# Idle score strips take quarter-products of PV as 32x32 tiles, in a two-layer attention and MLP kernel

## The chip, the cores and the metric

The kernel runs on one core of one Trainium2 chip. The metric is the device time in microseconds (us), median over the runs. The core's engines have queues of their own: PE (matmuls, with PEld for the weight loads), ACT (activations), DVE and POOL (elementwise work), SP (DMA issue).

## What is computed

Two times the same pair of blocks over x of 2048 rows by 512, in bf16, with the same weights: attention with 32 heads of 16, then an MLP of width 1792.

```
x = x + A(layernorm(x));  x = x + B(layernorm(x))        # twice
A: q, k, v = split(x @ wqkv);  p = softmax(q k^T / 4);  (p @ v) @ wo
B: gelu(x @ w1 + b1) @ w2 + b2
```

A head has only 16 dimensions, so the matmuls of attention are small and the exponentials many: 2 x 32 x 2048 x 2048 of them.

## The kernel before

The kernel is a planner in Python: generators (`scores`, `exps`, `pvs`, `solo`, `hpair`, ...) yield operations with costs, `_Sched.run` picks at each step the operation that can start first on its engine by a clock of its own, and the result is one fixed order of instructions for each engine, with semaphore waits. A table of weights, `ROWS`, holds settings of the planner's rules, and `PIECES` says which row holds in each hundredth of the program.

Attention goes in passes. A pass is a layer, a block of 512 queries and four heads, one in each quarter of 128 channels (in the last blocks 256 queries and eight heads; `setup_attention`). Its unit of work is a cell `(pass, kt, a)`: 128 keys, the head in quarter `a`, 512 columns. In all there are 4096 cells. A cell's score (`score`, line 1598 of before) is a matmul with 32 rows of weights and 128 columns on row strip `a` of the array (tile position `(32a, 0)`). A **score phase** (mode "S") issues scores on two to four different strips; mostly it is three: two for ACT and one for DVE. Each goes to a bank of PSUM of its own.

A cell's exponentials come from one of two places. On ACT (`exps`, line 2234) one activation takes two or three cells, that is 1024 or 1536 columns, and writes `pt`. On DVE (`dfirst`, line 1867) one operation per cell makes integers whose bits read as bf16 approximate the exponential, and two shifted copies (POOL, line 2097) refine it, so that a cell on DVE gives three products to be added, where a cell on ACT gives one.

A **product** multiplies 128 keys of `p` with 17 columns of `v` (16 dimensions and a column of ones for the softmax's sum), at tile `(0, 32a)`: 128 rows by 32 columns. `pvs` (line 2301) issues rounds of four of them, one on each quarter of columns, into the one PV bank (`PVB`), which stays open over a pass (mode "P"). The projections and the MLP (line 715) have the same 128x32 shape. Where the plan has PE idle, `fill` puts in matmuls without use (line 1586).

`next_act` and `next_d` choose the cells of a phase; `op.late` is called when a phase's start is known and may add cells (`attach`, `more`); `op.apart` holds matmuls that go out in the same phase under a semaphore step of their own. The planner charges a phase or a round `MM`, and `SW` at each change between modes S and P.

Of the kernel before, what the change touches and what calls it, by code (L numbers as in the profile page):

```python
# [63 lines left out]
KWAIT = (140, 230, 320)  # L64
KSTEP = 10
# [30 lines left out]
         "CLOSE",)  # L96
ROWS = (
# [42 lines left out]
)  # L140
PIECES = (4, 23, 28, 27, 28, 25, 25, 25, 23, 25, 20, 25, 25, 25, 20, 20, 20, 24, 15, 36, 36, 30, 31, 24, 24, 24, 33, 33, 24, 24, 24, 0, 0,
          5, 5, 37, 25, 25, 6, 25, 14, 18, 30, 30, 3, 35, 37, 5, 19, 19, 5, 20, 38, 41, 38, 35, 35, 35, 35, 24, 17, 17, 17, 14, 19, 7, 7, 7,
          18, 18, 18, 39, 39, 22, 15, 1, 41, 41, 39, 41, 39, 25, 25, 2, 2, 14, 23, 25, 25, 35, 35, 32, 32, 34, 36, 32, 38, 41, 41, 32)
# [193 lines left out]
class _Sched:  # L337
# [169 lines left out]
    def run(self):  # L507
        while True:
# [62 lines left out]
            for f, r, w in op.apart:  # L571
                ev = self.P.group(e, [f], r, w)
                self.end[ev] = start + cost + op.tail + LATENCY[e]
# [131 lines left out]
class _Plan:  # L705
# [746 lines left out]
    def setup_attention(self):  # L1452
# [40 lines left out]
        self.slots = [list(x) for x in SLOTS]  # L1493
        self.held, self.users = [len(x) for x in SLOTS], [0] * len(SLOTS)
        self.dmine = {c for q in self.dlist for c in q}
        self.ended, self.pvopen, self.pvwas, self.hold = False, False, False, set()
        self.rush = self.base[(NL - 1, self.segs[-1][-3])]
        self.duleft, self.open, self.starved, self.lend = {}, None, 0, 2
        self.tbusy, self.s.tbusy = set(), None
# [101 lines left out]
    def next_act(self, used=()):  # L1601
        while self.pa < len(self.pas):
            for q in (self.alist[self.pa], self.dlist[self.pa]):
                if q:
                    return q.pop(next((k for k, c in enumerate(q) if c[2] not in used), 0))
# [816 lines left out]
```

## Time and profile before

| | |
|---|---|
| median of three runs | 1375.13 us (1374.58 to 1377.1) |
| the profiled execution | 1374.89 us, span 1373.1 us |
| busy in the span | PE 1338.8, ACT 1349.0, DVE 1261.8, POOL 802.8 us |
| matmuls | 18168, and as many weight loads |
| ACT's exponentials | start 12.2 us to 1343.8 us into the span |

A run's time is a little over its span. Busy times of an engine join instructions that overlap: an activation's recorded length contains the end of the one before, and a matmul's end is modelled. So distances from start to start tell more than lengths.

### The profile page before, as it was taken

The numbers are of one execution on the slowest core, as the hardware profiler recorded it, in microseconds if no ns is written. First come the engines' busy times: TensorE is split into PE (matmuls) and PEld (weight loads), VectorE is DVE, ScalarE is ACT, GpSimd is POOL, SyncE is SP. The second block draws the span as 40 slices with busy tenths as digits, with TensorE's granted clock in tenths as the row PEclk, the third lists the DMA queues.
The fourth block names the chain that finished last, engine by engine and source line by source line (L and its number), as shares of the span: only waits on it lengthen the run. The fifth ranks groups of instructions, "written<-read, shape, count | busy, mean of one in ns | idle before, by whom it ended". The sixth has DMA issues, their size and how long they took to land.

```text
span 1373.1 us, 42332 instructions
## 1 busy us (share of the span) xinstructions
PE 1338.8 (98%) x18168; PEld 390.1 (28%) x18168; DVE 1261.8 (92%) x2504; ACT 1349.0 (98%) x1385; POOL 802.8 (58%) x1352
## 2 busy tenths in 40 slices
PE   9999999999999999999999999999999999999999
PEld 3222222222222222222222222222222222333446
DVE  8999999989999899998979899999999898999894
ACT  7999999999999999999999999999999999999995
POOL 1367667657665567665626666546656665765461
DMA  5300000123221221112451141100104314201112
GB/s 149 72 2 1 2 2 23 49 75 97 71 43 45 89 83 55 44 51 65 114 109 40 49 128 57 48 17 12 37 24 117 93 40 143 83 14 44 29 34 83
DMA packets 122296, 80.20 MB, mean 58 GB/s; under 512 B 36732, under 2 KB 121084, under 8 KB 122108
## 3 DMA queue, kind: packets, MB, share of 16 engines
q1 hardware_dynamic: 122108, 77.49, 20.6%
q8 instruction: 143, 2.34, 0.7%
q14 instruction: 45, 0.37, 0.1%
HBM read 65.67 MB, written 4.19 MB: 51 GB/s over the span
## 4 chain that ended last, share of the span: by engine, by line
ACT 83%; PE 10%; DVE 6%; DMA 1%; issue 0%
ACT pt L2234 70%; PE ps L715 5%; ACT kt L2234 3%; ACT g L1276 3%; PE ps L1598 3%; ACT v L2234 2%; PE ps L2301 2%; DVE dp L1867 2%; ACT q L2234 2%; DVE kt L1867 1%; ACT L2234 1%; ACT L1276 1%; ACT g L2234 1%; DVE stats L848 0%; DMA wr<-in_B_w_dram 0%; DMA wr<-in_A_wqkv_dram 0%
## 5 line engine op out<-in xcount | busy, mean ns | idle before, releaser
L2234 ACT ACTIVATE pt<-ps 128x1024 bf16<-128x1024 f32 (+1 forms) x1183 | 1142.7, 1176 | 2.0 <-PE ps L1598 1.6
L1598 PE MATMUL ps<-qp,kt 32*128 32x512 bf16 x4096 | 551.5, 384 | 16.6 <-ACT pt L2234 12.2
L2097 POOL INT64_ADD dp<-dp x732 | 440.2, 613 | 204.8 <-DVE dp L1867 123.1
L1867 DVE TENSOR_SCALAR dp<-ps 128x512 uint16<-128x512 f32 x733 | 483.3, 679 | 26.3 <-PE ps L1598 23.4
L1598 PEld LDWEIGHTS ps<-qp,kt 32*128 32x128 bf16 x4096 | 138.4, 91 | 569.7 <-ACT pt L2234 466.7
L2097 POOL INT64_ADD kt<-kt x320 | 190.1, 599 | 174.1 <-DVE kt L1867 93.6
L2301 PE MATMUL ps<-pt,v 128*17 128x512 bf16 (+1 forms) x2758 | 273.9, 359 | 1.4 <-ACT pt L2234 0.7
L1867 DVE TENSOR_SCALAR kt<-ps 128x512 uint16<-128x512 f32 x309 | 207.4, 683 | 23.4 <-PE ps L1598 20.8
L2301 PE MATMUL ps<-dp,vc 128*17 128x512 bf16 (+1 forms) x1652 | 220.7, 357 | 0.6 <-POOL xf L2097 0.4
L2301 PE MATMUL ps<-dp,v 128*17 128x512 bf16 (+1 forms) x826 | 139.1, 357 | 3.4 <-DVE xt L1076 2.4
L2097 POOL INT64_ADD v<-v x155 | 94.1, 611 | 71.7 <-DVE v L1867 35.8
L715 PE MATMUL ps<-xf,wr 128*32 128x512 bf16 (+1 forms) x1888 | 134.6, 366 | 0.5 <-DVE g L1258 0.4
L2301 PE MATMUL ps<-kt,vc 128*17 128x512 bf16 (+1 forms) x766 | 117.6, 340 | 1.0 <-POOL xf L2097 0.3
L1867 DVE TENSOR_SCALAR v<-ps 128x512 uint16<-128x512 f32 x154 | 102.8, 682 | 13.2 <-PE ps L1598 12.8
L715 PE MATMUL ps<-wr,g 128*32 128x512 bf16 x1408 | 108.1, 384 | 0.5 <-DVE dp L1867 0.2
L2301 PEld LDWEIGHTS ps<-pt,v 128*17 128x17 bf16 x2758 | 69.8, 88 | 74.5 <-issue 51.8
L2301 PE MATMUL ps<-kt,v 128*17 128x512 bf16 (+1 forms) x507 | 85.8, 350 | 1.7 <-DVE xt L1076 1.0
L2097 POOL INT64_ADD xf<-xf x78 | 46.5, 596 | 65.5 <-DVE xf L1867 40.3
L1258 DVE TENSOR_SCALAR g<-ps,hb1t 128x512 bf16<-128x512 f32 (+1 forms) x112 | 78.9, 706 | 1.0 <-PE ps L715 1.0
L2301 PEld LDWEIGHTS ps<-dp,vc 128*17 128x17 bf16 x1652 | 56.7, 88 | 42.0 <-issue 24.4
L2234 ACT ACTIVATE kt<-ps 128x1024 bf16<-128x1024 f32 (+1 forms) x60 | 63.4, 1189 | 0.0
L2301 PE MATMUL ps<-v,vc 128*17 128x512 bf16 x308 | 60.8, 381 | 0.0
(124 smaller groups left out, 1425.5 us busy)
## 6 DMA issues: line engine op xcount, KB each, us to landing
wr<-in_B_w_dram SPq DMA_DIRECT2D x174, 256.0 KB, 2.9
wr<-in_A_wqkv_dram SPq DMA_DIRECT2D x24, 256.0 KB, 3.3
x<-in_A_x_dram SPq DMA_DIRECT2D x7, 512.0 KB, 4.3
wr<-in_A_wo_dram SPq DMA_DIRECT2D x10, 256.0 KB, 3.7
kept<-x SPq DMA_DIRECT2D x4, 512.0 KB, 3.1
x<-kept SPq DMA_DIRECT2D x4, 512.0 KB, 4.4
out_dram<-x SPq DMA_DIRECT2D x16, 128.0 KB, 2.5
q<-in_B_w_dram SPq DMA_DIRECT2D x3, 512.0 KB, 4.5
```

The lines of the kernel that those rows point to most:

```text
L715: return [lambda e, a=a: e.matmul(out[32 * a:32 * a + 32, :], lhsT=lhsT[:, 32 * a:32 * a + 32], rhs=rhs, start=start, stop=stop, tile_posi ...
L1258: yield _Op("dve", 0.21 + n / 966, lambda e, fc=fc, pb=pb: e.tensor_scalar(T["G"][:, fc, q], pb, T["HB1T"][:, fc:fc + 1], None, op0=ALU.ad ...
L1276: lambda e, g=g: e.activation(out=g, in_=g, func=ACT.Gelu_apprx_tanh), reads=gk, writes=gk, prio=2)
L1598: return (lambda e: e.matmul(o, lhsT=lhsT, rhs=rhs, start=True, stop=True, tile_position=(32 * a, 0)), ["K%d.%d.%d" % (l, gb, kt // 4), "Q ...
L1867: yield _Op("dve", 0.682, lambda e: e.tensor_scalar(u, self.bank(b), E_SCALE, E_BIAS, op0=ALU.mult, op1=ALU.add), reads=["B.%d" % b], writ ...
L2097: op = _Op("pool", PFIX + PWORD * 128 * (hi - lo), lambda e: e.int64_add(dst, src, by * PACKED), reads=reads, writes=writes)
L2234: yield _Op("act", EXPC + 0.4267 * n, lambda e, src=src, dst=dst: e.activation(out=dst, in_=src, func=ACT.Exp, scale=0.25), reads=["B.%d" ...
L2301: op.fns.append(lambda e, o=o, lhsT=q[0][0][m], rhs=q[0][1][:, n * m:n * m + n], a=a, st=st, sp=sp: e.matmul(o, lhsT=lhsT, rhs=rhs, start= ...
```

## The change

A score phase mostly leaves a row strip idle. The change lets that strip do a quarter of four products: 32 of the 128 keys of one product in each of the four column quarters, four matmuls on 32x32 tiles at `(32r, 32a)`, accumulated into the open PV bank. Such four matmuls are called a **unit** here. Four units, on four different strips in four different phases, finish four products, a round of `pvs` before. `beside` makes units: at most one between two phases of another mode, and each waits on PE's own semaphore for the unit before it. `avoid` steers the choice of cells so that the strip left idle is one that a begun set of four still lacks. `pvs` issues what is left at the end of a pass as units alone. The table of settings gets a new column and more rows, and `PIECES` is chosen anew.

```diff
+PARTS = 2
+PLEFT = 7
+STEER = 1
...
-    (0.5, 0.3, 0.7, 0.2, 10, 10, 2, 6, 1, 1, 2, 2, 5, 0.3, 0.4, 2, 3.5, 24, 3, 4, 0.4, 1.0, 0, 1, 2, 3, 1, 2, 0.3, 2, 0.15, 0.0, 0.35,),
+    (0.5, 0.3, 0.7, 0.2, 10, 10, 2, 6, 1, 1, 2, 2, 5, 0.3, 0.4, 2, 3.5, 24, 3, 4, 0.4, 1.0, 0, 1, 2, 3, 1, 2, 0.3, 2, 0.15, 0.0, 0.35, 7,),
...
-            for f, r, w in op.apart:
+            for f, r, w, *order in op.apart:
+                for x in order:
+                    for y in x:
+                        self.P.wait(e, *y)
                 ev = self.P.group(e, [f], r, w)
+                for x in order:
+                    x[:] = [ev]
...
+    def avoid(self):
+        parts = self.cur["parts"] if self.cur and STEER else []
+        left = set.union(*[x["left"] for x in parts]) if parts else set()
+        return left if parts and (len(parts) == PARTS or not self.cur["more"]) and len(left) < 3 else set()
...
+    def beside(self, op, start, cells):
+        if self.s.mode != "S":
+            self.laid = False
+        cur = self.cur
+        if cur is None or self.laid or not all(cur["begun"]):
+            return
+        idle = [r for r in range(4) if all(c[2] != r for c in cells)]
+        if not idle:
+            return
+        cur["more"] = min(self.pvleft[k] for k in cur["cols"]) >= PLEFT
+        part = next((x for x in cur["parts"] if x["left"] & set(idle)), None)
+        if part is None and cur["more"] and len(cur["parts"]) < PARTS:
...
+        r = next(r for r in idle if r in part["left"])
+        part["left"].discard(r)
+        op.apart.append((self.quarter(cur, part, r, len(cur["parts"]) == 1 and not part["left"] and not any(self.pvleft[k] for k in cur["cols"])),
+                         part["keys"], ["B.%d" % cur["b"]], self.order))
+        self.laid = True
...
+    def quarter(self, cur, part, r, end):
+        bank, n = self.bank(cur["b"]), cur["n"]
+        row = slice(32 * r, 32 * r + 32)
+
+        def f(e):
+            for m in range(512 // n):
+                for a, ws, p in part["work"]:
+                    x = e.matmul(bank[32 * a:32 * a + 17, n * m:n * m + n], lhsT=ws[m][row, :], rhs=p[row, n * m:n * m + n], start=False, stop=end and m == 512 // n - 1,
+                                 tile_position=(32 * r, 32 * a))
+            return x
+        return f
...
+                for r in sorted(x["left"]):
+                    op = _Op("pe", MM, [self.quarter(cur, x, r, i == len(cur["parts"]) - 1 and r == max(x["left"]))], reads=x["keys"], writes=["B.%d" % b], prio=0.5, mode="S")
+                    op.late = lambda op, start: self.P.wait("pe", "pe", self.P.cnt["pe"])
+                    yield op
+                    self.order[:] = [("pe", self.P.cnt["pe"])]
```

Lines move: the scores stand at 1647 in the changed kernel (1598 before), the rounds of PV at 2440 (2301), projections and MLP at 763 (715), the fillers at 1635 (1586), ACT's exponentials at 2372 (2234), DVE's at 2004 (1867). The units are line 1724.

What the built programs hold, counted in their order of instructions:

| | before | after |
|---|---|---|
| scores (line 1598, 1647) | 4096 | 4096 |
| cells on ACT, in activations of two cells and of three | 2769 in 1200 + 123 | 2756 in 1210 + 112 |
| cells on DVE | 1327 | 1340 |
| matmuls of fillers in the 128x32 and 128x17 shapes | 404 | 604 |
| matmuls of units, units | 0 | 3728 in 828 (104 of them in two halves of 256 columns) |
| places where 128-row and 32-row tiles follow each other | 2730 | 2682 |
| matmuls in all | 18168 | 21296 |

On PE of before, in the stretch where the hidden layer of an MLP block runs beside attention (`xf,wr`), a score phase of three is followed directly by rounds of 128-row tiles.

```order
L1598 MATMUL ps<-qp,kt 128x512 x3
L715 MATMUL ps<-xf,wr 32x512 x8
L1598 MATMUL ps<-qp,kt 128x512 x3
L715 MATMUL ps<-xf,wr 32x512 x8
L1598 MATMUL ps<-qp,kt 128x512 x3
L2301 MATMUL ps<-pt,v 17x512 x8
L1598 MATMUL ps<-qp,kt 128x512 x3
```

On PE of the changed kernel at such a place, with the semaphores that an instruction waits for, four matmuls of a unit (line 1724) stand behind the three scores.

```order
L1647 MATMUL ps<-qp,kt 128x512 [waits s_act]
L1647 MATMUL ps<-qp,kt 128x512
L1647 MATMUL ps<-qp,kt 128x512 [waits s_dve]
L1724 MATMUL ps<-pt,v 17x512 [waits s_pe]
L1724 MATMUL ps<-pt,v 17x512 x3
L763 MATMUL ps<-xf,wr 32x512 x8
L1647 MATMUL ps<-qp,kt 128x512 [waits s_act]
L1647 MATMUL ps<-qp,kt 128x512
L1647 MATMUL ps<-qp,kt 128x512 [waits s_dve]
L1724 MATMUL ps<-pt,v 17x512 [waits s_pe]
L1724 MATMUL ps<-pt,v 17x512 x3
```

The unit comes between the scores and the MLP's rounds and brings one wait, on PE's own semaphore; the rounds that it stands for are gone from elsewhere in the pass.

The second place is on PE of the changed kernel at the end of a pass, where a set of four is not complete and its remaining units go out alone, behind the last rounds of line 2440 (with the zero columns of line 2448).

```order
L2440 MATMUL ps<-pt,v 17x512 x3
L2448 MATMUL ps<-b2row,zero 17x512
L1724 MATMUL ps<-pt,v 17x512 [waits s_pe]
L1724 MATMUL ps<-pt,v 17x512 x3
L1724 MATMUL ps<-pt,v 17x512 [waits s_pe]
L1724 MATMUL ps<-pt,v 17x512 x3
L1647 MATMUL ps<-qp,kt 128x512 [waits s_act]
```

Here each unit waits for what PE issued directly before it; there are 15 such units in the program, and the next scores stand behind them.

More of the change, by code (lines that the diff above doesn't have):

```diff
@@ L64 @@
 KWAIT = (140, 230, 320)
+PARTS = 2
+PLEFT = 7
+PAGE = 10
+STEER = 1
 KSTEP = 10
@@ L95 @@
          "ALONE", "AHEAD", "PSHIFT", "QUEUE", "SOLO", "BACK", "SIDE", "BOTH", "DMAX", "GMAX", "PMORE", "DUMORE", "GRACE", "PPS", "WAIT", "SOFT",
-         "CLOSE",)
+         "CLOSE", "PLEFT",)
 ROWS = (
[42 rows of a table removed]
-)
-PIECES = (4, 23, 28, 27, 28, 25, 25, 25, 23, 25, 20, 25, 25, 25, 20, 20, 20, 24, 15, 36, 36, 30, 31, 24, 24, 24, 33, 33, 24, 24, 24, 0, 0,
-          5, 5, 37, 25, 25, 6, 25, 14, 18, 30, 30, 3, 35, 37, 5, 19, 19, 5, 20, 38, 41, 38, 35, 35, 35, 35, 24, 17, 17, 17, 14, 19, 7, 7, 7,
-          18, 18, 18, 39, 39, 22, 15, 1, 41, 41, 39, 41, 39, 25, 25, 2, 2, 14, 23, 25, 25, 35, 35, 32, 32, 34, 36, 32, 38, 41, 41, 32)
[80 rows of a table added]
+)
+PIECES = (75, 70, 35, 29, 64, 73, 68, 68, 25, 25, 73, 53, 73, 73, 70, 54, 73, 76, 32, 20, 58, 25, 71, 53, 53, 79, 53, 66, 25, 25, 53, 44,
+          35, 35, 35, 79, 79, 58, 19, 14, 76, 44, 44, 74, 41, 32, 78, 71, 71, 71, 71, 43, 71, 74, 54, 66, 71, 53, 58, 7, 53, 53, 57, 57, 64,
+          25, 29, 29, 29, 53, 79, 39, 76, 20, 15, 45, 45, 67, 25, 35, 35, 34, 78, 68, 68, 68, 79, 68, 25, 17, 41, 14, 71, 71, 66, 66, 66,
+          35, 33, 45)
 CLOSE = 0.35
@@ L1496, in setup_attention @@
         self.ended, self.pvopen, self.pvwas, self.hold = False, False, False, set()
+        self.cur, self.laid, self.units_done, self.order = None, False, 0, []
         self.rush = self.base[(NL - 1, self.segs[-1][-3])]
@@ L1599, in score @@
                 ["K%d.%d.%d" % (l, gb, kt // 4), "QP.%d" % qs] + ["K0.0.0.b"] * ((l, gb) == (0, 0) and kt in (2, 3)))
+    def avoid(self):
+        parts = self.cur["parts"] if self.cur and STEER else []
+        left = set.union(*[x["left"] for x in parts]) if parts else set()
+        return left if parts and (len(parts) == PARTS or not self.cur["more"]) and len(left) < 3 else set()
     def next_act(self, used=()):
+        most = self.avoid() | set(used)
         while self.pa < len(self.pas):
@@ L1604, in next_act @@
                 if q:
-                    return q.pop(next((k for k, c in enumerate(q) if c[2] not in used), 0))
+                    k = next((k for k, c in enumerate(q) if c[2] not in most), None)
+                    return q.pop(next((k for k, c in enumerate(q) if c[2] not in used), 0) if k is None else k)
             self.pa += 1
         return None
+    def beside(self, op, start, cells):
[10 more added lines that the diff above has]
+        if part is None and cur["more"] and len(cur["parts"]) < PARTS:
+            got = []
+            for k in cur["cols"]:
+                for q in (self.aq[k], self.dq[k]):
+                    i = next((i for i, x in enumerate(q) if ("V", cur["l"], x[5], x[5] // 4) in self.s.tokens and self.s.landed(x[2]) <= start
+                              and not any(y[0] == "seen" for y in x[3])), None)
+                    if i is not None:
+                        got.append((k, q, i))
+                        break
+            if len(got) < 4 or cur["wait"] and not self.rest(got, start):
+                return
+            part = {"left": set(range(4)), "work": [], "keys": [], "back": []}
+            for k, q, i in got:
+                x = q.pop(i)
+                part["work"].append((k[1], x[0], x[1]))
+                part["keys"] += x[2]
+                part["back"] += x[3]
+                self.pvleft[k] -= x[4]
+            cur["parts"].append(part)
+        if part is None:
+            return
+        r = next(r for r in idle if r in part["left"])
[3 more added lines that the diff above has]
+        self.laid = True
+        self.units_done += 1
+        if not part["left"]:
+            cur["parts"].remove(part)
+            for pool, x in self.freed(part["back"]):
+                self.s.pools[self.s.route(pool, x)].append(x)
@@ new lines, in rest @@
+    def rest(self, got, start):
+        took = [id(q[i]) for _, q, i in got]
+        for k in self.cur["cols"]:
+            for q in (self.aq[k], self.dq[k]):
+                x = next((x for x in q if id(x) not in took), None)
+                if x is not None and ("V", self.cur["l"], x[5], x[5] // 4) in self.s.tokens and self.s.landed(x[2]) <= start:
+                    return True
+        return False
+    def quarter(self, cur, part, r, end):
[8 more added lines that the diff above has]
+        return f
@@ L1609, in next_d, with freed @@
+    def freed(self, back):
+        for pool, r in back:
+            if pool == "seen":
+                r[0]["seen"][r[1]] += 1
+                continue
+            if pool == "du":
+                self.duleft[r] -= 1
+                if self.duleft[r]:
+                    continue
+            if pool == "pl":
+                if not self.drop(*r):
+                    continue
+                r = r[1]
+            yield pool, r
     def next_d(self, used, start, pop=True):
@@ L1623, in next_d @@
                 break
-            for k, (_, kt, a) in enumerate(self.dlist[pi]):
+            most = self.avoid() | set(used)
+            for k, (_, kt, a) in sorted(enumerate(self.dlist[pi]), key=lambda x: x[1][2] in most):
                 if a not in used and ("vc", self.visit[pi]) in tok and ("K", l, gb, kt // 4) in tok:
@@ L1842, in scores @@
             op = _Op("pe", MM, fns, reads=reads, writes=writes, mode="S", slack=max(SLACK, ahead - LATE))
-            op.late = lambda op, start, sl=sl, cells=cells, extra=extra: (self.attach(op, start, cells, extra), self.more(op, start, cells, extra, sl))
+            op.late = lambda op, start, sl=sl, cells=cells, extra=extra: (self.attach(op, start, cells, extra), self.more(op, start, cells, extra, sl),
+                                                                                     self.beside(op, start, cells + [x[0] for x in extra]))
             op.soft = self.slots[sl][2] if len(cells) == 2 and len(self.slots[sl]) > 2 else None
@@ L1898, in solo @@
             self.join(op, d, b, extra)
+            op.late = lambda op, start, d=d: self.beside(op, start, [d])
             yield op
@@ L2259, in pvs @@
             begun = [False] * 4
+            self.cur = cur = {"b": b, "l": l, "n": n, "cols": cols, "begun": begun, "parts": [], "more": True, "wait": False}
             def have(k):
@@ L2294, in build @@
                     rounds += 1
-                    end = all(self.pvleft[k] == sum(q[0][4] for x, q in got if x == k) for k in cols)
+                    end = not cur["parts"] and all(self.pvleft[k] == sum(q[0][4] for x, q in got if x == k) for k in cols)
                     for m in range(512 // n):
@@ L2332, in pvs @@
                 op.late, op.back = build, []
+                cur["wait"] = True
                 yield op
-                back = op.back
-                for pool, r in back:
-                    if pool == "seen":
-                        r[0]["seen"][r[1]] += 1
-                        continue
-                    if pool == "du":
-                        self.duleft[r] -= 1
-                        if self.duleft[r]:
-                            continue
-                    if pool == "pl":
-                        if not self.drop(*r):
-                            continue
-                        r = r[1]
+                cur["wait"] = False
+                for pool, r in self.freed(op.back):
+                    yield ("rel", pool, r)
+            cur["more"] = False
+            yield ("cond", lambda cur=cur: not cur["parts"] or self.ended or self.s.force or self.s.clock["act"] < self.s.clock["pe"] + 0.3)
+            self.cur = None
+            for i, x in enumerate(cur["parts"]):
+                self.s.force = False
+                for r in sorted(x["left"]):
[3 more added lines that the diff above has]
+                    self.order[:] = [("pe", self.P.cnt["pe"])]
+                for pool, r in self.freed(x["back"]):
                     yield ("rel", pool, r)
```

120 rows, old and new, of the table ROWS are left out of this document.

## The prediction

> **What bounds the kernel now.** I read the page first, then the busy time by stages, then the two bound engines row by row in the timeline. The page's shares leave two candidates:
>
> ```profile
> span 1373.1 us, 42332 instructions
> PE 1338.8 (98%) x18168; PEld 390.1 (28%) x18168; DVE 1261.8 (92%) x2504; ACT 1349.0 (98%) x1385; POOL 802.8 (58%) x1352
> ACT 83%; PE 10%; DVE 6%; DMA 1%; issue 0%
> L2234 ACT ACTIVATE pt<-ps 128x1024 bf16<-128x1024 f32 (+1 forms) x1183 | 1142.7, 1176 | 2.0 <-PE ps L1598 1.6
> L1867 DVE TENSOR_SCALAR dp<-ps 128x512 uint16<-128x512 f32 x733 | 483.3, 679 | 26.3 <-PE ps L1598 23.4
> ```
>
> ACT and PE are both at 98%, but the chain that ended last runs through ACT for 83% of the span, and ACT's largest group waited for PE only 2.0 us in all. The stages (columns: stretch, its length, then PE, PEld, DVE, ACT, POOL busy) say the same more sharply:
>
> ```profile
> 12.00:350.00 338.00, 330.05 (x4131) 88.92 (x4126) 321.65 (x646) 337.68 (x344) 200.13 (x338) 1.00 0.15 39
> 350.00:680.00 330.00, 324.25 (x4143) 85.71 (x4139) 311.46 (x603) 329.77 (x344) 207.55 (x345) 1.00 0.25 69
> 680.00:1010.00 330.00, 320.60 (x4063) 84.65 (x4063) 304.05 (x592) 329.37 (x335) 187.59 (x318) 1.00 0.20 53
> 1010.00:1345.00 335.00, 328.47 (x5126) 109.57 (x5122) 303.76 (x580) 334.64 (x336) 204.63 (x345) 1.00 0.22 63
> ```
>
> From 12 to 1345 us ACT is busy 1331.5 of 1333 us, PE 1303.4. The waits agree: a score's weight load waits for ACT to free its bank 1113 times.
>
> ```profile
> PEld ps L1598 <- ACT pt L2234: 466.7, 1113, 1.8
> ```
>
> So ACT bounds the middle, with PE close behind. What ACT pays per activation is the distance from start to start:
>
> ```profile
> 299.05 7.47 ACT L2234 ACTIVATE pt<-ps 128x1024 bf16<-128x1024 f32 x8
> ...
> 676.42 1.51 ACT L2234 ACTIVATE g<-ps 128x1536 bf16<-128x1536 f32 x1
> 677.75 2.44 ACT L2234 ACTIVATE pt<-ps 128x1024 bf16<-128x1024 f32 x2
> ...
> L2234 ACT ACTIVATE pt<-ps 128x1024 bf16<-128x1024 f32 x1079 | 1017.7, 1142 | 0.6 <-PE ps L1598 0.2
> L2234 ACT ACTIVATE pt<-ps 128x1536 bf16<-128x1536 f32 x104 | 155.4, 1529 | 1.4 <-PE ps L1598 1.4
> ```
>
> Eight activations of two cells last 7.47 us, the last one about 1.14: (7.47 - 1.14) / 7 = 0.904 us each. One of three cells goes from 676.42 to 677.75: 1.33 us. With the order's counts, 1200 x 0.904 + 123 x 1.33 = 1248 us. Gelu (43.9 us) and 15 table loads (19.3 us) lie in the same stretch, which leaves about 20 of its 1333 us for late starts:
>
> ```profile
> L1276 ACT ACTIVATE g<-g 128x3584 bf16<-128x3584 bf16 x14 | 43.9, 3182 | 0.1
> L1276 ACT ACT_TABLE_LOAD x8 | 10.3, 1283 | 0.1
> L2234 ACT ACT_TABLE_LOAD x7 | 9.0, 1283 | 0.1
> ```
>
> PE's prices come from the same place:
>
> ```profile
> 676.43 0.39 PE L2301 MATMUL ps<-pt,v 128*17 128x512 bf16 x4
> 676.75 0.39 PE L1598 MATMUL ps<-qp,kt 32*128 32x512 bf16 x3
> 677.08 0.82 PE L2301 MATMUL ps<-pt,v 128*17 128x512 bf16 x10
> 677.52 0.60 PE L2301 MATMUL ps<-kt,v 128*17 128x512 bf16 x6
> 678.05 0.39 PE L1598 MATMUL ps<-qp,kt 32*128 32x512 bf16 x4
> 678.37 0.39 PE L2301 MATMUL ps<-kt,v 128*17 128x512 bf16 x2
> ```
>
> One round of PV and the change to scores take 676.75 - 676.43 = 0.32 us; four rounds and the change take 678.05 - 677.08 = 0.97. A round is thus (0.97 - 0.32) / 3 = 0.217 us and a change of tile shape 0.10. A score phase of three strips takes 0.33 with the change behind it, and one of four strips 0.32: a fourth strip in the same shape costs at most 0.01 us.
>
> **The change, part by part.** *Rounds removed.* 828 units are 207 whole rounds of PV: 207 x 0.217 = 44.9 us off PE. There are 48 fewer changes of shape: 4.8 us. *Rounds added.* 13 more cells on DVE need two more products each: 26 products, 6.5 rounds, 1.4 us. The fillers' 200 more matmuls are 50 rounds, but they stand where the plan has PE idle, so I cost them at nothing; if that idle time isn't there on the chip they cost 10.9 us.
>
> *The unit itself* is not in this trace: no 32x32 tile, and no two shapes at once. Between what ends can it lie? The nearest row below is the fourth strip, at most 0.01 us. The far end is a unit that runs alone: a round and one more change, 0.217 + 0.10 = 0.32 us. I take 0.01 (828 x 0.01 = 8.3 us), because a unit's rows are a strip that the scores beside it don't use. The trace shows four row strips running together (the x4 of 678.05) and four column quarters running together (the x4 of 676.43); the unit needs both at once. Below nothing it cannot be, since its matmuls come on top of the phase.
>
> By the Trainium skill, "TensorE: Matmul & The Clock Gate", Part 3, a weight load overlaps matmuls in flight where its row group differs, and 16 tiles of 32x32 were measured at 10.6 times the speed of one after another. By that a unit would be as cheap as a fourth strip; no run shown here has such tiles.
>
> *The unit's wait* is on PE's own semaphore. For nearly all of the 739 units that have one, a PV round and a phase lie between (0.64 us by the rows above), longer than a matmul's recorded 0.39, so I cost it at nothing. Were it to hold, the rounds behind it on PE would be late, and through them the next scores that ACT and DVE wait for. The 15 units at a pass's end that wait for the instruction just ahead pay up to 0.39 - 0.217 = 0.17 us each, 2.6 in all.
>
> *Sum for PE:* -44.9 - 4.8 + 1.4 + 8.3 + 2.6 = -37 us. PE gets looser, but it isn't the bound.
>
> *ACT* is: 11 activations of three cells fewer, 10 of two more: -11 x 1.33 + 10 x 0.904 = -5.6 us. By the grouped rows (155.4 / 104 = 1.49, 1017.7 / 1079 = 0.94) it would be -7.0; those lengths contain overlap, so I take 5.6.
>
> *DVE* gets 13 cells at 483.3 / 733 = 0.66 us: 8.6 us, hidden in its 111 idle us. It and POOL's shifts lie beside ACT; if that cover fails, the 5.6 us are given back. *Late starts:* about 20 us; a looser PE should give back a little, and I take 1 us (from nothing to 5). SP's queue and the head and tail around the exponentials keep their work.
>
> The profiled execution took 1374.89 us (its span 1373.1 and 1.8 around it), 0.2 below the median of 1375.13. The forecast against the median: 1375.13 - 5.6 - 1 = 1368.5 us.
>
> **Rivals.** *A unit drains PE.* Each unit stands alone and costs 0.32 us: 828 x 0.32 = 265 us, less 44.9 + 4.8, plus 1.4 + 2.6: +219 on PE. Its slack is 1373.1 - 1338.8 = 34 us idle and the fillers:
>
> ```profile
> L1586 PE MATMUL ps<-b2row 128*32 128x512 bf16 x324 | 26.9, 384 | 0.1
> L1586 PE MATMUL ps<-b2row,zero 128*17 128x512 bf16 x80 | 7.3, 383 | 0.0
> ```
>
> 404 matmuls, 101 rounds, 22 us. PE's own work is then 1373 - 34 - 22 + 219 = 1536 us, plus some of the idle time: about 1550. For it: every one of the 2730 changes between 128-row and 32-row tiles goes one after the other, 0.10 us late, and the trace has no exception. Against it: in every one of them the newcomer needed rows that were in use, so the trace can't tell a drain from occupied rows. This is the case on the other side; it decides from (44.9 + 4.8) / 828 = 0.06 us per unit, where PE is as full as before. The Trainium skill, "TensorEngine Tiling (Array Packing)", Key Properties, has it as a rule: changing the tiling mode, not just the tile, drains TensorE; and 32x128 to 32x32 is such a change in its list.
>
> *A unit starts late,* its weights not loaded behind the scores: the 0.10 us of a change, but streams together. 828 x 0.10 = 83, less 49.7, plus 4: +37 us on PE, of which 22 us of fillers and some of the 34 idle us take up most. From 1375 to 1392, say 1384.
>
> *The gain goes nowhere.* The 13 cells move but POOL or DVE bring products later, and the freed rounds become fillers, as 50 of 207 do in the order: 1375. For it: ACT waited so little for PE that PE's relief alone buys almost nothing. Against it: fewer activations are certain.
>
> **How the numbers follow.** Chances: forecast 0.62 (1364 to 1373), gain goes nowhere 0.08, late units 0.11, drain 0.19. The drain gets that much because the nearest rows for a change of shape all show it paid; the forecast more, because those rows share rows of the array and the unit doesn't. The range leaves out the drain alone: from 1364 (late starts shrink by 5) to 1392 (late units' upper end), which holds 0.81. About 0.2% (2.7 us) is what a measurement can tell here. Faster by more: the forecast less 0.02 at its edge, 0.60. Within: 0.02, 0.07 of the second and 0.02 of the late units, 0.11. Slower: 0.01 + 0.09 + 0.19 = 0.29.
>
> **What would show it.** Right: in the timeline a unit (line 1724) starts within 0.02 us of its scores and the round behind them still 0.32 to 0.34 us after the scores' start; ACT's exponentials are 1322 and end some 6 us earlier, their spacing still 0.904; PE's fillers are more. Wrong by the drain: the unit starts 0.32 us after the scores, the next round 0.64, ACT's busy share falls below 90%. Wrong by late units: the unit starts about 0.1 us behind the scores and ACT shows gaps before the scores of line 1647.

## The result, and the profile after

| | median | runs | granted TensorE clock |
|---|---|---|---|
| before | 1375.14 us | 1374.58 to 1377.10 (4 runs) | 1.000 in the profile |
| after | 1646.02 us | 1636.22 to 1657.09 (4 runs) | 0.966 to 0.979 |

The ratio is 1.197, with a 95% interval of 1.188 to 1.206. The forecast was 1368.5 us; the change costs 271 us. Two runs further down, 1673.07 and 1738.00 us, lie over 1.5% above the fastest of their kernels; they are listed and are in no ratio.

The head of the page of after (profiled execution: 1657.09 us) shows which engine bounds it now. Third line: the chain that ended last, by engine; then the group of ACT's exponentials and the group of the units (busy time and mean length, then idle time ahead of them).

```profile
span 1655.3 us, 48620 instructions
PE 1624.2 (98%) x21296; PEld 459.7 (28%) x21296; DVE 1314.2 (79%) x2520; ACT 1412.7 (85%) x1384; POOL 812.1 (49%) x1373
PE 83%; ACT 11%; DVE 4%; DMA 1%; issue 0%; POOL 0%; POOLq 0%
L2372 ACT ACTIVATE pt<-ps 128x1024 bf16<-128x1024 f32 (+1 forms) x1259 | 1266.3, 1071 | 211.4 <-PE ps L1647 116.4
L1724 PE MATMUL ps<-pt,v 32*17 32x512 bf16 (+1 forms) x3512 | 322.3, 364 | 1.0
```

PE and ACT have changed places. ACT's share of the chain fell from 83% to 11%, its busy share from 98% to 85%, and its exponentials now wait 211 us where they waited 2. ACT's waits name what it waits for: 325 times the scores, and 148 times a unit.

```profile
ACT pt L2372 <- PE ps L1647: 116.4, 325, 2.6
ACT pt L2372 <- PE ps L1724: 85.7, 148, 2.0
```

The second kind is another path on which a late unit costs time. Such an activation overwrites the P that the unit still reads, so it waits for the unit's semaphore step (161 activations of the program do; in before, 5 wait for a round of PV in this way). By the trace it starts 0.76 us after a score of its phase, where those that wait for the scores alone start 0.42 us after it.

The timeline of PE in after (start, length, line and tile shape) gives the price directly. It is the row that the prediction said to look at:

```profile
800.38 0.39 PE L1647 MATMUL ps<-qp,kt 32*128 32x512 bf16 x3
800.70 0.39 PE L1724 MATMUL ps<-pt,v 32*17 32x512 bf16 x4
801.02 0.39 PE L2440 MATMUL ps<-pt,v 128*17 128x512 bf16 x1
...
804.15 0.39 PE L1647 MATMUL ps<-qp,kt 32*128 32x512 bf16 x3
804.48 0.39 PE L1724 MATMUL ps<-pt,v 32*17 32x512 bf16 x4
804.79 0.61 PE L763 MATMUL ps<-wr,g 128*32 128x512 bf16 x8
```

A unit starts 0.32 us after its scores, and the round behind it 0.64 us after them. In the whole trace the median distance from a phase of three scores to its unit is 0.321 us (727 places) and from a unit to the next round 0.319 us (657 places). Within a unit the four matmuls start 3 to 4 ns apart: they do run together, but not beside the scores.

The stages of after show a second thing, which the prediction had not considered (columns: stretch, length, then busy time of PE, PEld, DVE, ACT, POOL; PE's granted clock is the third number from the end):

```profile
388.00:401.00 13.00, 13.00 (x99) 2.11 (x96) 6.60 (x17) 7.24 (x7) 5.52 (x9) 0.52 0.01 1
411.00:476.00 65.00, 64.91 (x482) 10.73 (x478) 31.46 (x56) 32.20 (x32) 20.63 (x35) 0.50 0.12 37
476.00:560.00 84.00, 83.27 (x1040) 22.15 (x1036) 72.30 (x133) 74.02 (x75) 45.26 (x77) 1.00 0.12 30
...
1561.00:1585.00 24.00, 24.00 (x239) 5.05 (x235) 10.64 (x19) 12.33 (x13) 5.24 (x9) 0.50 0.04 12
```

In some stretches the clock is half: from 411 to 476 us PE issues 7.4 matmuls per us, right behind that 12.4. In the profiled run these stretches add up to about 113 us. Span times clock takes them out: 1599, 1601, 1600 and 1597 us in the four runs. So by this estimate after needs about 1599 us of span at full clock, and 34 to 56 us are lost to the clock.

### The profile page after: what moved, and what is told of

Read it like the earlier page. It is cut to its first block, busy times and chain, and to the rows that moved or that the text cites. A ratio compares the mean times of both kernels' runs of the same rounds, so it can differ in the third digit from the quotient of the medians.

```text
span 1655.3 us, 48620 instructions
## 1 busy us (share of the span) xinstructions
PE 1624.2 (98%) x21296; PEld 459.7 (28%) x21296; DVE 1314.2 (79%) x2520; ACT 1412.7 (85%) x1384; POOL 812.1 (49%) x1373
## 4 chain that ended last, share of the span: by engine, by line
PE 83%; ACT 11%; DVE 4%; DMA 1%; issue 0%; POOL 0%; POOLq 0%
PE ps L1647 24%; PE ps L2440 21%; PE ps L763 20%; PE ps L1724 16%; ACT pt L2372 10%; PE ps L1635 1%; DMA wr<-in_B_w_dram 1%; DVE dp L2004 1%; ACT g L1324 1%; DVE kt L2004 1%; DVE xt L1124 0%; DVE v L2004 0%; PE ps L2448 0%; DVE stats L896 0%; DVE v L1120 0%
## 5 line engine op out<-in xcount | busy, mean ns | idle before, releaser
L2372 ACT ACTIVATE pt<-ps 128x1024 bf16<-128x1024 f32 (+1 forms) x1259 | 1266.3, 1071 | 211.4 <-PE ps L1647 116.4
L2004 DVE TENSOR_SCALAR dp<-ps 128x512 uint16<-128x512 f32 x750 | 505.5, 684 | 136.6 <-PE ps L1647 131.7
L1647 PE MATMUL ps<-qp,kt 32*128 32x512 bf16 x4096 | 578.9, 393 | 13.1 <-ACT pt L2372 9.0
L1724 PE MATMUL ps<-pt,v 32*17 32x512 bf16 (+1 forms) x3512 | 322.3, 364 | 1.0
L2440 PE MATMUL ps<-dp,vc 128*17 128x512 bf16 (+1 forms) x1682 | 240.0, 370 | 0.3 <-ACT pt L2372 0.2
L2440 PE MATMUL ps<-pt,v 128*17 128x512 bf16 (+1 forms) x2058 | 235.2, 364 | 1.6 <-ACT pt L2372 0.7
L2440 PE MATMUL ps<-dp,v 128*17 128x512 bf16 (+1 forms) x841 | 159.5, 368 | 3.9 <-DVE xt L1124 1.7
L1724 PEld LDWEIGHTS ps<-pt,v 32*17 32x17 bf16 x3512 | 75.1, 82 | 188.7 <-PE ps L2440 83.5
L2440 PE MATMUL ps<-kt,v 128*17 128x512 bf16 (+1 forms) x428 | 76.4, 346 | 1.1 <-DVE xt L1124 0.7
L2440 PEld LDWEIGHTS ps<-pt,v 128*17 128x17 bf16 x2058 | 58.6, 88 | 64.2 <-issue 44.6
```

Source lines behind the costliest of these rows:

```text
L1647: return (lambda e: e.matmul(o, lhsT=lhsT, rhs=rhs, start=True, stop=True, tile_position=(32 * a, 0)), ["K%d.%d.%d" % (l, gb, kt // 4), "Q ...
L1724: x = e.matmul(bank[32 * a:32 * a + 17, n * m:n * m + n], lhsT=ws[m][row, :], rhs=p[row, n * m:n * m + n], start=False, stop=end and m == ...
L2004: yield _Op("dve", 0.682, lambda e: e.tensor_scalar(u, self.bank(b), E_SCALE, E_BIAS, op0=ALU.mult, op1=ALU.add), reads=["B.%d" % b], writ ...
L2372: yield _Op("act", EXPC + 0.4267 * n, lambda e, src=src, dst=dst: e.activation(out=dst, in_=src, func=ACT.Exp, scale=0.25), reads=["B.%d" ...
L2440: op.fns.append(lambda e, o=o, lhsT=q[0][0][m], rhs=q[0][1][:, n * m:n * m + n], a=a, st=st, sp=sp: e.matmul(o, lhsT=lhsT, rhs=rhs, start= ...
```

## Experiments

**Theories.** *A*: any change of tile shape makes PE finish what is in flight, whichever rows it uses. *B*: the unit is late for another reason, its wait on PE's own semaphore, its weight loads, or the number of tiles.

The trace of after already speaks against the wait: 87 units have none, and they start at the same 0.32 us as the 732 with one that could be paired with their scores.

In the last place of that timeline (804.15) the weight loads (PEld) start 0.32 us apart too, and the unit's matmuls follow its loads by 0.01 us. So the loads are held back together with the matmuls, and aren't what fills the time.

```profile
804.15 0.10 PEld L1647 LDWEIGHTS ps<-qp,kt 32*128 32x128 bf16 x3 [0.42 <-issue]
804.47 0.09 PEld L1724 LDWEIGHTS ps<-pt,v 32*17 32x17 bf16 x4 [0.23 <-PE ps L763]
```

**The unit in the shape of the scores.** The unit is one 32x128 matmul on the same strip, into the same bank, with the same wait; every pass begins with a round of zero weights, to start the rows that it adds to.

```diff
-            for m in range(512 // n):
-                for a, ws, p in part["work"]:
-                    x = e.matmul(bank[32 * a:32 * a + 17, ...], lhsT=ws[m][row, :], ..., tile_position=(32 * r, 32 * a))
+            p = part["work"][0][2]
+            return e.matmul(bank[:, :], lhsT=self.T["IDENT"][row, :], rhs=p[row, :], start=False, stop=end, tile_position=(32 * r, 0))
...
+                if not any(begun):
+                    for a in range(4):
+                        op.fns.append(lambda e, ...: e.matmul(
+                            o, lhsT=T["ZERO"][:, 0:32], rhs=..., start=True, stop=False, tile_position=(0, 32 * a)))
```

> Each unit becomes one matmul on a 32x128 tile, the scores' own shape, on the same idle strip, into the same PV bank, behind the same wait; its weights are the identity, so the sums of PV change. So that all 128 rows of the bank take part, each pass starts with a round of zero weights (68 rounds, at 0.217 us 15 us of PE that the plan doesn't know). Theory 1 (a change of tile shape makes PE finish what runs, whatever rows are in use): nothing changes shape here, the unit starts within 0.02 us of the scores, the rounds behind at 0.33 us, and the time is 1369 to 1385. Theory 2 (the PV bank, or the wait on PE's own semaphore, holds the unit back): the unit still starts 0.32 us after the scores and the time stays above 1600.

Measured: 1381.70 us (ratio 1.0046, 1.0031 to 1.0061). PE's timeline of this kernel:

```profile
801.28 0.39 PE L1647 MATMUL ps<-qp,kt 32*128 32x512 bf16 x3
801.29 0.39 PE L1723 MATMUL ps<-pt,ident 32*128 32x512 bf16 x1
801.61 0.39 PE L2443 MATMUL ps<-dp,vc 128*17 128x512 bf16 x4
```

The unit starts 3 ns behind the last score (10 ns behind the first, 0.01 in these rows), and the next round comes 0.32 us after them, as without a unit. This is the price that the prediction took, for a unit that keeps the shape. PE's order, the strip, the bank and the wait are those of after, so none of these makes the unit late. The chain that ended last is PE for 47% of the span and ACT for 40%.

**The scores in the shape of the unit.** In a phase with a unit, each score is four 32x32 tiles on its strip.

```diff
-        return (lambda e: e.matmul(o, lhsT=lhsT, rhs=rhs, start=True, stop=True, tile_position=(32 * a, 0)),
+            for c in range(4):
+                x = e.matmul(o[32 * c:32 * c + 32, :], lhsT=lhsT[:, 32 * c:32 * c + 32], rhs=rhs, start=True, stop=True, tile_position=(32 * a, 32 * c))
...
+        op.fns = [f.quads for f in op.fns]
```

> In phases that have a unit, and there alone, each score goes out as four 32x32 tiles side by side on its strip, so that scores and unit have one shape; everything is still computed. Theory 1 (change of shape): the unit joins the scores, its cost falls from 0.32 us to the start-to-start spread, 3.3 ns for each of some 13 more matmuls (0.04 us), and the time is 1366 to 1385, as ACT bounds again. Theory 2 (32-column tiles on one strip collide with scores that take all columns of another, or the PV bank holds the unit back): still about 0.32 us per unit and over 1600.

Measured: 1393.55 us (ratio 1.0132, 1.0116 to 1.0149), above the 1366 to 1385 that were expected. PE's timeline, and the chain that ended last:

```profile
800.77 0.42 PE L1652 MATMUL ps<-qp,kt 32*32 32x512 bf16 x12
800.81 0.39 PE L1737 MATMUL ps<-pt,v 32*17 32x512 bf16 x4
801.12 0.83 PE L763 MATMUL ps<-wr,g 128*32 128x512 bf16 x12
```

```profile
PE 54%; ACT 39%; DVE 5%; DMA 1%; issue 0%
```

Twelve score tiles and the unit's four go out 3.3 ns apart, and the next round starts 0.359 us after the first score instead of 0.321 (medians). The real unit on its real strip joins its scores once the shapes agree, for 0.038 us. Its weight loads, the same as in after, start 0.04 us behind the scores' first load, so they don't make the unit late either. That ACT bounds again, as the expectation had it, is not what the chain shows: PE has more of it than ACT. That the Trainium skill measured 16 such tiles at 10.6 times the speed of one after another ("TensorE: Matmul & The Clock Gate", Part 3) fits this, within one shape.

**Another shape that differs.** As the first experiment, but the unit is two 32x64 matmuls side by side.

```diff
-            return e.matmul(bank[:, :], lhsT=self.T["IDENT"][row, :], rhs=p[row, :], start=False, stop=end, tile_position=(32 * r, 0))
+            for c in (0, 64):
+                x = e.matmul(bank[c:c + 64, :], lhsT=self.T["IDENT"][row, c:c + 64], rhs=p[row, :], start=False, stop=end, tile_position=(32 * r, c))
```

> As the kernel with units of 32x128, but each unit is two matmuls on 32x64 tiles side by side on the idle strip; the weights are the identity, so the sums of PV change, and each pass starts with a round of zero weights. Theory 1 (any change of tile shape makes PE finish what runs): the unit starts 0.32 us after the scores again, and the time is above 1580. Theory 1a (only a change to 32 columns, the shape of the PV rounds, does so): the unit starts within 0.02 us and the time is that of the 32x128 units, about 1382.

Measured: 1665.76 us (two runs, 1656.96 and 1674.55; ratio 1.2115, 1.1963 to 1.2266), clock 0.970 and 0.982. PE's timeline:

```profile
800.80 0.39 PE L1647 MATMUL ps<-qp,kt 32*128 32x512 bf16 x1
801.12 0.40 PE L1724 MATMUL ps<-pt,ident 32*64 32x512 bf16 x2
801.45 0.38 PE L2445 MATMUL ps<-dp,vc 128*17 128x512 bf16 x1
```

Two matmuls instead of one, and the unit is 0.32 us late again. So neither the number of tiles nor the 32x32 tile as such matters; A stands, for two shapes that differ from the scores'.

**No units, and half of them.** In these the planner works with other phases and picks its order anew, so that they differ from after in more than the units.

```diff
-PARTS = 2
+PARTS = 0
```

> The changed kernel with no units (PARTS = 0), so only the new table rows, the new choice of rows and the planner's order for it. Both theories: no unit, so no 0.32 us; the freed 45 us of PE are back. Time 1370 to 1385: the order picked for units is a little worse without them. If it is above 1400, a part of the loss is the new order's.

Measured: 1401.68 us (1401.47 to 1401.79; ratio 1.0192, 1.0177 to 1.0207), clock 1.0, above the 1370 to 1385 that were expected. The settings that were picked for units are 26.6 us worse than those of before when no unit goes out. This is not the order's part in the loss of after, since the planner makes another order here: the first experiment has PE's order of after and takes 1381.70.

```diff
-        if cur is None or self.laid or not all(cur["begun"]):
+        if cur is None or self.laid or not all(cur["begun"]) or self.pv % 2:
```

> Units in every second pass only, about 414 of 828. If each unit costs 0.32 us of a PE that is full, the time lies near the middle between no units and all: about 1490 to 1520, and the granted clock falls less. If the loss came from something that happens once (the clock, the order), it wouldn't halve.

Measured: 1514.05 us (ratio 1.1009, 1.0987 to 1.1031), 404 units, clock 0.999 and 1.000. From none to 404 units the time rises by 112.4 us, 0.278 each; a unit at 0.32 that saves a quarter of a round (0.054) should add 0.266. From 404 to 828 units the span at full clock rises by another 87 us, from 1512 to 1599, 0.205 each. So the loss grows with the units and doesn't happen once; it is not in strict proportion, and the three orders differ in more than units (their fillers are 656, 820 and 604 matmuls). The clock does not fall with half of the units.

**What the rest of the sum was worth.** The first experiment with two rounds of zero weights at the start of a pass instead of one. The trace counts 336 more matmuls, which are 84 rounds and not the 68 of the text on record.

```diff
-                    for a in range(4):
+                    for a, st in [(a, st) for st in (True, False) for a in range(4)]:
```

> The kernel with the unit as one 32x128 matmul, whose passes now begin with two rounds of zero weights instead of one: 68 more rounds of four matmuls, in the same order. The unit matmul adds 32 rows of P themselves and not P times V, as in the first of these kernels. It prices one set of zero rounds, which stands in the way of reading the rest of the sum from the 1381.7 us of that kernel. If PE bounds that kernel where the rounds stand, 68 x 0.217 = 15 us more, 1396 to 1397, and the same kernel without zero rounds would be near 1367, the time on record plus nothing: the unit's price was then the only wrong term. If ACT covers half of them, 1387 to 1391, and the kernel without zero rounds would be near 1374 to 1376, no gain: then the sum had a second error, of some 6 us, even with a free unit.

Measured: 1399.08 us (1398.20 to 1399.76), somewhat above the 1396 to 1397 of the expectation's first case and 17.4 more than with one set; 84 x 0.217 is 18.2. PE pays nearly all of it. By a straight line the kernel of the first experiment without its one set would be near 1381.7 - 17.4 = 1364. That is an estimate, and a low one: no kernel without zero rounds ran, and the first set can have cost less than the second if ACT covered part of it. So this run can't show that the rest of the sum was sound. It shows that PE's work is paid in a kernel whose units are cheap.

**What the fillers do.** First the fillers of after stream 8 columns instead of 512 (those few at the start keep theirs), in the same order; then each is issued twice, and four times.

```diff
+                o, thin = o[:, 0:8], rhs[:, 0:8]
...
-        for a in range(1 if mode == "F" else 4):
+        for a in (0,) * 2 if mode == "F" else (0, 1, 2, 3) * 2:
```

> The changed kernel with the same order, but its fillers (604 matmuls of lines in the 128x32 shape, 151 rounds) stream 8 columns instead of 512; they compute nothing that is used. Theory 1: PE bounds the changed kernel all the way, so work that stood in planned idle time now costs its full 0.2 us a round: about 30 us less at full clock, 1600 - 30 = 1570, if the granted clock doesn't fall more than in the changed kernel. Theory 3 (fillers cost nothing, as the prediction had it): no change from about 1600 at full clock. With fewer busy columns the clock may fall for longer, which would show in the clock's rows and is to be taken off.

> The changed kernel with every filler issued twice in place, so some 140 more rounds of matmuls that stream 128 rows by 512 columns, and nothing else changed. It asks whether the granted clock falls because little of the array streams. Each more round costs 0.217 us on PE, about 30 us in all, so at full clock the span goes from about 1598 to about 1628. If the clock falls for want of streaming, it is granted more here than in the changed kernel's 0.966 to 0.979: 0.985 or above, and the time is 1630 to 1655, no slower than the changed kernel's 1636 to 1657 for 30 us more work. If the fall has nothing to do with what streams, the clock is 0.966 to 0.979 again and the time 1662 to 1685.

> The changed kernel with every filler issued four times in place. The kernel with each issued twice left the clock's cause open: its two runs had 0.992 and 0.968, and span times clock 1626 and 1618, so that one more set of the 168 filler rounds cost about 23 us at full clock. Three more sets make the span at full clock 1598 + 3 x 23 = 1667. If the clock falls for want of streaming, all runs have 0.985 or more and take 1667 to 1695. If it falls by chance or for another reason, the runs have 0.966 to 0.979 again, as the changed kernel, and take 1703 to 1727.

| fillers | time of each run, us | clock of each | span x clock, us |
|---|---|---|---|
| 8 columns | 1699.13, 1711.73 | 0.926, 0.916 | 1572, 1566 |
| as in after | 1657.09, 1640.01, 1636.22, 1652.03 | 0.966, 0.977, 0.979, 0.968 | 1597 to 1601 |
| twice | 1640.49, 1673.07 | 0.992, 0.968 | 1626, 1618 |
| four times | 1699.70, 1699.72, 1721.13, 1738.00 | 0.998, 0.998, 0.983, 0.972 | 1688 to 1694 |

The row of granted clock of the profiled runs, in 40 slices, with 8 columns:

```profile
PEclk9999995999995899998999999979958999966999
```

of after:

```profile
PEclk9999999997579999999999999999999999999889
```

and with fillers four times:

```profile
PEclk9999999999999999999999999999999999999999
```

Two readings. By the means of the last column, thin fillers save 30 us, a second set costs 22 and each further set 35, where 168 rounds x 0.217 are 36: once PE bounds the kernel, fillers are paid for the most part. (With four times the fillers the expectation had 1667 at full clock, and 1688 to 1694 came out.) And with thin fillers the clock falls more: both runs with 8 columns lose 125 us and more to it, those of after 34 to 56. More fillers don't settle the cause. Twice the fillers have one run at 0.992 and one at 0.968; of the four runs with four times, two lose 3 us, the others 29 and 49, and 0.983 and 0.972 miss the 0.985 that was expected of every run. So thin fillers were seen with a lower clock, in two runs; that want of streaming is the cause of its fall in after was not shown.

No kernel here beats before.

## Why the prediction was wrong

**The step that failed is the price of the unit.** It was bracketed by 0.01 and 0.32 us, and I took 0.01 "because a unit's rows are a strip that the scores beside it don't use". The measured price is 0.32, the far end. 828 x 0.32 = 265 us instead of 8.3. The ground for the choice, that rows and not shapes are what waits, is what the first three experiments contradict: the same strip costs 3 ns in the scores' shape, 0.038 us when the scores take the unit's shape, and 0.32 us in the two other shapes. The rival had the rule right, and so had the Trainium skill in "TensorEngine Tiling (Array Packing)", Key Properties: changing the tiling mode drains TensorE. All 2730 changes in the trace of before agreed with it; I set them aside because none of them tested free rows. A pattern without an exception in 2730 rows deserved more than 0.19.

**The drain rival's mechanism was right and its time, 1550, was too low.** Two of its terms failed:

- *Slack.* It let 34 us of idle PE and 22 us of fillers absorb the cost. Neither did. PE idles 1655.3 - 1624.2 = 31 us in after. The fillers are instructions in a fixed order, and there are 200 more of them, 10.9 us. Without that slack the rival's own terms give 1373.1 + 219 + 10.9 = 1603 us of span; span times clock measures 1599. That they agree so closely is in part luck, since the zero columns counted below (5.8 us) are not in that sum.
- *The clock.* No term for it was in the prediction. It adds 34 to 56 us, and 1599 becomes 1634 to 1655.

**"They stand where the plan has PE idle, so I cost them at nothing".** The fillers' 10.9 us hung on the same wrong price: the plan's idle places were worked out for a cheap unit. With a PE that is never idle they cost what they stream.

**"PE gets looser, but it isn't the bound" failed too,** even where the unit is cheap. The kernel with the scores in the unit's shape computes everything, has no zero rounds, and pays 828 x 0.038 = 31 us for units where the sum had 8.3. By the prediction's own sum PE would still be 14 us looser than before, and the forecast still near 1368.5. It measured 1393.55, with PE at 54% of the chain, where before had 10%. Two terms of the sum were at nothing:

- *Fillers,* 10.9 us, as above.
- *Zero columns.* PV's rounds have more empty places, which line 2448 fills: 228 matmuls, 122 in before (line 2309). No term has these 106, at four to a round 26.5 rounds or 5.8 us.

With both paid, PE is some 3 us fuller than before, not looser. That leaves about 16 of the 18 us by which this kernel is slower than before; what they are is not shown.

**ACT's -5.6 us** can't be seen in after, because ACT waits 211 us, and no kernel got a lower time from it. The program has 11 activations of three cells fewer and 10 of two more, as the sum says. But the last exponential starts at 1343.8 us in before, at 1352.7 with 32x128 units and at 1363.9 with the scores in the unit's shape: later starts ate the saving, where the forecast had late starts shrink by 1 us.

**What held.** The unit's wait on its own engine costs nothing: the 3 ns of the first experiment are measured with it. A round at 0.217 us and a change of shape at 0.10 are the same in after (unit to round 0.32). "The gain goes nowhere" and "a unit starts late" (0.10 us) are both out: the unit starts 0.32 us behind its scores.

## What to carry to other kernels

In these runs free rows of the array were usable only by a matmul of the same tile shape as those in flight: before filling an idle strip, ask which shape the neighbour has, and count a different one as a phase of its own. When the rows of a trace all show a cost and none shows the exception that a plan needs, take the cost as the forecast and the exception as the rival. Slack that is made of issued instructions doesn't give way when its engine becomes the bound. And where two engines are both at 98%, relief for one is worth only what its whole order really loses, empty places of its rounds included.

## What the runs showed of the hardware

In this kernel a change of tile shape made the next matmul and its weight load wait for those in flight even where they shared no row strip: 0.32 us for 32x32 and 32x64 tiles behind 32x128 ones on a free strip, against 3 ns for a 32x128 tile there. Sixteen 32x32 tiles of two kinds start 3.3 ns apart and take 0.359 us with the change behind them.

The granted clock can fall to half while PE is busy without a gap: 0.50 from 411 to 476 us of after, with PE busy 64.91 of 65 us. Its mean was lower when matmuls between were made to stream less (0.916 and 0.926, against 0.966 to 0.979), and it fell not at all with half the units (0.999 and 1.000). What sets it off is open.
